# More places for the scheduler in a block pair, and a later earliest moment for the weighted sums of v, in a fused attention and feed-forward kernel

## The chip, the cores and the metric

The kernel runs on one core of one Trainium2 chip. The metric is the device time in microseconds, the median of several runs. TensorE is called PE here (its weight loads PEld), VectorE is DVE, ScalarE is ACT, GpSimd is POOL, and SyncE, which issues DMAs, is SP.

## The reference

Softmax attention over 8 batches, 12 heads, 448 positions and a head size of 64 is followed by a feed-forward layer with a leaky ReLU on the 3584 tokens that it gives:

```python
scores = np.matmul(q, k.transpose(0, 1, 3, 2)) / np.sqrt(64)      # q, k, v: (8, 12, 448, 64)
attn = np.exp(scores - scores.max(-1, keepdims=True))
attn = attn / (attn.sum(-1, keepdims=True) + 1e-09)
x = np.matmul(attn, v).transpose(0, 2, 1, 3).reshape(3584, 768)
h = x @ w_in                                                      # w_in: (768, 2048)
out = np.maximum(0.01 * h, h) @ w_out                             # w_out: (2048, 768)
```

## The kernel before

**Attention.** The work is cut into 48 units, each a pair of heads of one batch, and each unit into four chunks of 112 keys. `scores` (matmuls at L271) writes the scores of a chunk for both heads into one of three PSUM slots (`slots`, taken in turn by `next_slot`); `expo` (L280, ACT) reads the slot and writes the exponentials `e` to SBUF. `rows` is the weighted sum of v for a whole unit: 32 small matmuls (L789) into the next slot, then a reciprocal (L795) and a product (L796) on DVE. The rows of x that come of it are transposed by a DMA on SP's queue (`turn`, L237) into `xT`. `burst` issues the scores of three chunks and their exponentials, so it needs all three slots. GpSimd casts q, k and v for later units (L170, L172) and issues their loads (L141), and SP also transposes q and k (into `qkT`); `advance` issues one step of each, and what it may issue depends on `chunk` (chunks begun) and `rows_done` (units whose weighted sum is issued).

**Feed-forward.** The tokens are cut at `cuts` = 0, 640, 1152, 1664, 2176, 2688, 3072 and 3584 into seven stages. In each of stages 1 to 6 `hidden(i)` makes h by a seven-product scheme on halves of the matrices (matmuls at L469), and `second(i)` multiplies h by w_out in pairs of blocks of 128 tokens. `block_pair` does a pair with seven products of eight matmuls of 384 columns (L541), into two PSUM banks `b` and `a` in turn; each product is followed by a copy (`keep`, L546) or an addition (`join`, L549) that empties its bank, and the first two by a subtraction on h (L553, L558). In a stage of fewer than 512 tokens, and in the last one, the first copy of the first pair is done by ACT, all others by DVE. Stage 0 is different: its hidden part is `head` and `neck`, and its first pair is a `plain_pair` (L606).

**The sums on x.** The seven-product scheme of `hidden(i + 1)` wants sums and differences of x, which `mix_x_part` makes on DVE (L416): four subtractions for the first two of three parts of k, then four for the third. In the stage where the tokens begin at the start of `xT`'s ring (stage 3) six small copies (L404) go ahead of them. `hidden` needs the third of each four for its fifth and sixth group of matmuls. `second(i)` issues them between the products if it can: `fresh` is the moment of the planner's clock from which they may go, 7.0 after the weighted sums that they depend on were placed. What has not been issued by the end of the pairs is issued behind them. In `hidden` there is one slot for weighted sums, and two of them are issued in a stage, after the second and the sixth group of matmuls.

**The order.** All of it is fixed when the program is built. `block_pair` and `plain_pair` are generators that `yield` at places; at each place `second(i)` calls `place`, which decides by a small model of times (`model`: the clock `now`, ACT's end `act`, when each slot is `free`, when a unit's exponentials are `ready`) whether a burst or weighted sums are issued there. It tries a burst first, and then a weighted sum where `calm` allows. `plan` = 9, 8, 8, 8, 8, 5, 0 says how many bursts each stage does. The tests on the model are these:

```python
x <= now + 0.05 + 0.2 * j for j, x in enumerate(at)              # a burst, slots j = 0, 1, 2
at[0] <= now + 0.05 and ready.get(u, 0) <= now + 0.05            # a weighted sum of unit u
```

Of the kernel before, what the change touches and what calls it, by code (L numbers as in the profile page):

```python
# [16 lines left out]
def kernel(  # L17
# [20 lines left out]
    NU = B * HP  # L38
# [3 lines left out]
    NR = len(cuts) - 1  # L42
    HEAD = S
    need = [HP * -(-t // S) for t in cuts]
# [59 lines left out]
    MH = MD // 2  # L104
# [17 lines left out]
    for t in (w_in_mix, w_mix):  # L122
        t = t.rearrange("p x k n -> p (x k n)")
# [301 lines left out]
    def token(i, x):  # L425

        return KEEP * P if x == KEEP else cuts[i] + x * P
# [96 lines left out]
    def block_pair(i, c):  # L524

        lo, hi = slice(0, MH), slice(MH, MD)
        x1, x2 = spots(i)[1][c]
        one, two = ts(x1, P), ts(x2, P)
        s3 = h_mix[:, :, c]
        t2, t3, t4 = (w_mix[:, x] for x in range(3))  # L530
        t1 = w_out_sb[:, lo, NW:]
        left, right = slice(0, NW), slice(NW, DM)
        o1 = o_pool.tile([P, DM], F32, name="o")
        o2 = o_pool.tile([P, DM], F32, name="o")
        b, a = banks

        def product(ps, x, w, first=False, cols=slice(0, NW)):
            for m in range(MH):
                if m == MH // 2:
                    yield  # L540
                nc.tensor.matmul(  # L541
                    ps[:, cols], x[:, m], w[:, m], start=(first and m == 0), stop=(m == MH - 1), skip_group_check=True,
                )

        def keep(o, at, ps, by=nc.vector.tensor_copy):
            by(o[:, at], ps[:, :NW])  # L546

        def join(o, at, ps):
            nc.vector.tensor_add(o[:, at], o[:, at], ps[:, :NW])  # L549

        yield
        yield from product(b, h[:, lo, one], w_out_sb[:, lo, left], first=True)
        nc.vector.tensor_sub(h[:, lo, one], h[:, lo, two], h[:, lo, one])  # L553
        short = cuts[i + 1] - cuts[i] < 4 * P
        keep(o1, left, b, nc.scalar.copy if c == 0 and (short or i + 1 == NR) else nc.vector.tensor_copy)
        yield
        yield from product(a, h[:, hi, one], w_out_sb[:, hi, left], first=True)
        nc.vector.tensor_sub(h[:, hi, one], h[:, hi, one], h[:, lo, one])  # L558
        join(o1, left, a)
        yield  # L560
        yield from product(b, h[:, lo, one], t2)
        keep(o1, right, b)
        yield
        yield from product(a, h[:, lo, two], t1, first=True)
        keep(o2, right, a)
        yield
        yield from product(b, s3, t3)
        join(o2, right, b)
        yield
        t0 = token(i, x2)  # L570
        last = t0 + P == B * S
        if last:
            nc.vector.tensor_copy(o2[:, NW // 2:NW], b[:, NW // 2:NW])
            store(o1, token(i, x1), left)
            store(o2, t0, right)
        yield from product(a, h[:, hi, one], w_out_sb[:, hi, right])
        join(o1, right, a)
        store(o1, token(i, x1), right if last else slice(0, DM))
        yield
        if last:  # L580
            w1, w2 = slice(0, NW // 2), slice(NW // 2, NW)
            yield from product(b, h[:, hi, two], t4[:, :, w1], cols=w1)
            nc.vector.tensor_copy(o2[:, w1], b[:, w1])
            store(o2, t0, w1, (nc.scalar, nc.sync))
            end = slots[0][:, 0]
            yield from product(end, h[:, hi, two], t4[:, :, w2], first=True, cols=w2)
            nc.vector.tensor_add(o2[:, w2], o2[:, w2], end[:, w2])
            store(o2, t0, w2, (nc.scalar, nc.sync))
            return
        yield from product(b, h[:, hi, two], t4)  # L590
        keep(o2, left, b)
        store(o2, t0)
        banks.reverse()
# [276 lines left out]
    model = {"now": 0.0, "act": 0.0, "free": {}, "ready": {}}  # L870

    def place(i, want, soon=0, full=True, calm=True, first=False, lazy=0, keen=NU, cap=NU):

        free, ready = model["free"], model["ready"]
        done, state = 0, 0
        while True:
            settle_x(model["now"])
            now = model["now"]
            last = divmod(chunk + 2, NSC)[0]
            blocked = rows_done <= min(last, NU - 1) - NE  # L880
            u = rows_done
            whole = u < chunk // NSC
            at = [free.get(id(x), 0.0) for x in slots]
            u = to["pe"]
            if full and max(want, soon) > done and u <= min(last, NPE - 1) and state == 0:
                transposes(u)
                to["pe"] += 1
                state = 1
                model["now"] += 0.45
                continue  # L890
            if want > done and state < 2 and turned(last) and not blocked and len(slots) == 3 and all(
                x <= now + 0.05 + 0.2 * j for j, x in enumerate(at)
            ):
                state = 2
                order = list(slots)
                start = chunk
                burst(lazy)
                if first:
                    feed(start // 3)
                done += 1  # L900
                for x, t in enumerate(order[:chunk - start]):
                    model["act"] = max(model["act"], now + 0.45 + 0.2 * x) + 0.8
                    free[id(t)] = model["act"] + (0.15, 0.15 + 0.5 * (lazy > 1), 0.15 + 0.5 * lazy)[x]
                    if (start + x) % NSC == NSC - 1:
                        ready[(start + x) // NSC] = model["act"] + 0.1
                model["now"] = now + 0.78
                continue
            u = to["pe"]
            if first and full and state == 0 and u < min(NPE - 1, to["cast"] - 1) and u - NQ < chunk // NSC and model["act"] <= now + 0.6:
                transposes(u)  # L910
                to["pe"] += 1
                state = 1
                model["now"] += 0.45
                continue
            u = rows_done
            if calm and whole and not (lazy and late) and at[0] <= now + 0.05 and ready.get(u, 0) <= now + 0.05 and (
                u <= (chunk + 5) // NSC - NE or u < keen
            ) and u < cap:
                t = slots[0]
                rows()  # L920
                if first:
                    pay()
                model["now"] = now + 1.08
                free[id(t)] = now + 2.33
                continue
            return done

    def second(i):

        x_sums = [mix_x_part(i + 1, slice(0, 2)), mix_x_part(i + 1, slice(2, 3))] if i + 1 < NR else []  # L930
        fresh, summed = [None, None], [i + 1 == NR] * 2
        left = plan[i]
        for c in range(len(spots(i)[1])):
            whole = c < plain(i)
            for x, _ in enumerate((plain_pair if whole else block_pair)(i, c)):
                if x % 2 == 0:
                    advance()
                if c or x:
                    model["now"] += 0.65
                left -= place(i, left, calm=whole or x not in (1, 3), keen=need[min(i + 2, NR)], cap=NU if all(summed) else need[i + 2])  # L940
                if whole and x in (1, 3, 5, 7):
                    mix_h(i, x - 1)
                if whole and x in (8, 9, 11, 13, 15):
                    next(outs)
                if i == 0 and c and x % 2:
                    next(ins, None)
                for y in range(2):
                    if fresh[y] is None and i + 1 < NR and rows_done >= need[i + 2] - 1 + y:
                        fresh[y] = model["now"] + 7.0
                for y, todo in enumerate(x_sums):  # L950
                    if fresh[y] is not None and fresh[y] <= model["now"] and not summed[y]:
                        summed[y] = next(todo, 0) is not None
                        if not summed[y]:
                            break
        assert left == 0 or chunk == NU * NSC, (i, left)
        assert i + 1 == NR or rows_done >= need[i + 2], (i, rows_done)
        for todo in x_sums:
            for _ in todo:
                pass
# [62 lines left out]
```

## Time and profile before

| what | value |
|---|---|
| median of 3 runs | 392.66 us (391.87 to 393.14) |
| the profiled execution | 389.6 us, its span 387.8 us |
| PE busy | 379.8 us, 98% |
| ACT busy | 265.3 us, 68% |
| DVE busy | 234.2 us, 60% |
| POOL busy | 142.9 us, 37% |
| mean granted clock of PE | 0.995 |
| stage 0's block pairs | from 75.2 to 107.9 us |
| hidden parts of stages 1 to 6 start at | 107.9, 157.2, 206.5, 255.7, 305.0, 347.3 us |
| block pairs of stages 1 to 6 start at | 128.3, 177.6, 226.9, 276.1, 320.9, 365.7 us |

A line of the page names the engine, the line of the program and what is written and read. Matmuls overlap, so the time of one is read from start to start, and the duration shown for one is longer. The time "idle before" names what ended an engine's wait.

### The profile page before, as it was taken

To read this page: it belongs to the slowest core of one execution; us is meant where nothing else is said; L and a number is where in the kernel's file an instruction comes from. 1 tells how busy PE (TensorE), PEld (TensorE's weight loads), DVE (VectorE), ACT (ScalarE), POOL (GpSimd) and SP (SyncE) were. 2 spreads that over 40 slices of the span, in tenths; PEclk is the share of its full clock that TensorE was granted. 3 is DMA by queue.
4 is the path that set the end of the run, shared out by engine and by line. 5 is a ranking of instruction groups with operands and counts; after the bars stand their busy time and mean duration, and the time that the engine had idled before them with its cause. 6 is when DMAs were issued, how large, how long until landed. Compare 5 with 4: busy or idle time off the path is not lost.

```text
span 387.8 us, 10006 instructions
## 1 busy us (share of the span) xinstructions
PE 379.8 (98%) x4093; PEld 260.6 (67%) x4093; DVE 234.2 (60%) x489; ACT 265.3 (68%) x391; POOL 142.9 (37%) x222
## 2 busy tenths in 40 slices
PE   7899999999999999999999999999999999999996
PEld 3665657755588655886558865578655795568854
DVE  3564767575767646657466574575745665464854
ACT  6898885767747877587776877758776677708700
POOL 8798820876545443620435304354042000000000
PEclk9899999999999999999999999999999999999999
DMA  8999999899997958991599913999138600421023
GB/s 129 198 200 203 184 200 173 110 132 211 132 133 115 147 99 141 204 127 25 84 153 164 162 34 62 174 148 183 29 51 174 138 18 3 107 55 51 3 75 89
DMA packets 93246, 46.75 MB, mean 121 GB/s; under 512 B 51856, under 2 KB 89872, under 8 KB 93200
## 3 DMA queue, kind: packets, MB, share of 16 engines
q0 software_dynamic: 38224, 22.58, 47.6%
q1 hardware_dynamic: 54912, 23.50, 32.4%
q8 instruction: 32, 0.52, 0.6%
q14 instruction: 14, 0.11, 0.1%
q10 hardware_dynamic: 64, 0.02, 0.0%
HBM read 45.61 MB, written 11.01 MB: 146 GB/s over the span
## 4 chain that ended last, share of the span: by engine, by line
PE 92%; DMA 3%; DVE 2%; POOL 1%; issue 1%; ACT 1%; POOLq 0%; DVEq 0%; ACTq 0%
PE g L541 30%; PE g L469 14%; PE sc L469 14%; PE sc L789 11%; PE sc L271 10%; PE g L352 4%; PE g L606 3%; PE g L647 2%; PE g L290 2%; DMA w_in_mix<-in_k_dram 2%; DMA xT<-x 1%; PE g L254 1%; POOL w_in_mix L141 1%; PE sc L352 1%; PE g L317 1%
## 5 line engine op out<-in xcount | busy, mean ns | idle before, releaser
L280 ACT ACTIVATE e<-sc 112x896 bf16<-112x896 f32 x192 | 163.2, 918 | 48.2 <-PE sc L271 48.0
L541 PEld LDWEIGHTS <-h 128*128 128x128 bf16 x632 | 57.1, 98 | 45.0 <-issue 13.3
L541 PE MATMUL g<-w_out_sb,h 128*128 128x384 bf16 x416 | 78.7, 326 | 0.0
L458 ACT ACTIVATE h<-c 128x512 bf16<-128x512 f32 (+1 forms) x72 | 43.5, 611 | 25.8 <-DVE c L484 16.8
L469 PEld LDWEIGHTS <-w_in_sb 128*128 128x128 bf16 x576 | 54.3, 98 | 6.2 <-issue 0.3
L170 POOL COPY qkb<-fq 112x512 bf16<-112x512 bf16 x38 | 26.9, 707 | 72.1 <-DMA qkT<-qkb 32.1
L789 PEld LDWEIGHTS <-e 112*128 112x128 bf16 x1344 | 46.5, 98 | 8.7 <-ACT e L280 7.4
L172 POOL COPY v<-fv 112x512 bf16<-112x512 bf16 x38 | 25.2, 672 | 69.8 <-PE sc L789 69.0
L271 PE MATMUL sc<-qkT 64*128 64x448 bf16 x384 | 50.0, 356 | 0.9 <-DVE qkT L260 0.7
L789 PE MATMUL sc<-v,e 112*128 112x65 bf16 x1344 | 50.1, 194 | 0.4 <-ACT e L280 0.4
L469 PEld LDWEIGHTS <-w_in_mix 128*128 128x128 bf16 x432 | 41.2, 98 | 4.1
L541 PE MATMUL g<-w_mix,h 128*128 128x384 bf16 (+1 forms) x208 | 38.3, 323 | 0.2 <-DVE o L549 0.2
L546 DVE COPY o<-g 128x384 f32<-128x384 f32 x49 | 27.1, 553 | 18.6 <-PE g L541 18.0
L795 DVE RECIPROCAL rec<-sc 112x8 f32<-112x8 f32 x42 | 8.7, 207 | 46.3 <-PE sc L789 41.3
L271 PEld LDWEIGHTS <-qkT 64*128 64x128 bf16 x384 | 15.0, 94 | 26.3 <-issue 18.3
L170 POOL COPY qkb<-fk 112x512 bf16<-112x512 bf16 x38 | 25.1, 660 | 17.3 <-DMA fk<-in_k_dram 17.2
L549 DVE TENSOR_TENSOR o<-o,g 128x384 f32<-128x384 f32 x39 | 21.5, 551 | 15.0 <-PE g L541 14.9
L796 DVE TENSOR_TENSOR x<-sc,rec 112x512 bf16<-112x512 f32 x42 | 29.0, 691 | 1.5
L469 PE MATMUL g<-xT,w_in_sb 128*128 128x256 bf16 (+1 forms) x216 | 28.5, 268 | 0.1
L469 PE MATMUL sc<-xT,w_in_sb 128*128 128x256 bf16 (+1 forms) x216 | 28.5, 268 | 0.0
L541 PE MATMUL g<-w_mix,hmix 128*128 128x384 bf16 x104 | 19.9, 326 | 0.0
L469 PE MATMUL g<-x_mix,w_in_mix 128*128 128x256 bf16 (+1 forms) x144 | 19.0, 268 | 0.0
(102 smaller groups left out, 480.2 us busy)
## 6 DMA issues: line engine op xcount, KB each, us to landing
fq<-in_q_dram POOLq DMA_DIRECT2D x19, 224.0 KB, 6.7
fk<-in_k_dram POOLq DMA_DIRECT2D x19, 224.0 KB, 7.3
fv<-in_v_dram POOLq DMA_DIRECT2D x19, 224.0 KB, 5.9
w_in_sb<-in_moe_w_in_dram POOLq DMA_DIRECT2D x4, 768.0 KB, 11.6
w_out_sb<-in_moe_w_out_dram POOLq DMA_DIRECT2D x4, 768.0 KB, 18.6
out_dram<-o SPq DMA_DIRECT2D x7, 336.0 KB, 4.7
out_dram<-o SPq DMA_DIRECT2D x8, 288.0 KB, 3.5
out_dram<-o SPq DMA_DIRECT2D x7, 240.0 KB, 3.4
```

The costliest lines, as they stand in the source:

```text
L170: by(qk_sb[u][:, x].rearrange("p so h d -> p h so d"), f)
L172: by(v_sb[u % NV][:, :, :, :D], f)
L271: nc.tensor.matmul(ps[:, j, :S], t[j * D:(j + 1) * D, S + c * SC:S + c * SC + P], t[j * D:(j + 1) * D, :S], start=True, stop=True,)
L280: nc.scalar.activation(e[:, :, c, :], sc_t.pop((u, c))[:SC, :, :S], AX.Exp, scale=scale)
L352: nc.tensor.matmul(open_t[m][:, :n], w_in_sb[:, kk, ts(m, P)], xT[:, kk, at:at + n], start=(fresh and kk == kks[0]), stop=(kk == KD - 1),)
L458: nc.scalar.activation(hs[:, m:m + 2, cols], x.rearrange("p (m t) -> p m t", m=2), AX.Prelu, alpha=0.01)
L469: nc.tensor.matmul(ps[:, j * nh:(j + 1) * nh], w[:, kk, ts(j, P)], x[:, kk], start=(first and j == 0 and kk == 0), stop=(kk == KH - 1), sk ...
L541: nc.tensor.matmul(ps[:, cols], x[:, m], w[:, m], start=(first and m == 0), stop=(m == MH - 1), skip_group_check=True,)
L546: by(o[:, at], ps[:, :NW])
L549: nc.vector.tensor_add(o[:, at], o[:, at], ps[:, :NW])
L789: nc.tensor.matmul(ps[:, j, qc, :], e[:, at:at + P], vt[:, j, c, :], start=(c == 0), stop=(c == NSC - 1),)
L796: nc.vector.tensor_mul(x_t[u].rearrange("p q j d -> p j q d"), ps[:SC, :, :, :D], rec.to_broadcast([SC, 2, NSC, D]))
```

## The change

It has three parts. In `block_pair` a product yields ahead of its third, fifth and seventh matmul, where it yielded ahead of its fifth alone, so that a pair has 28 places in place of 14. `second(i)` is adapted to it: in block pairs the planner's clock advances by 0.325 at a place in place of 0.65, and `advance`, `ins`, the subtractions of `x_sums` and the places forbidden to weighted sums are bound to the new numbers of the places. In `place` the first slot of a burst is held free 0.3 after the model's end of its exponential, where it was 0.15; the weighted sum of v takes that slot.

```diff
@@ block_pair
         def product(ps, x, w, first=False, cols=slice(0, NW)):
             for m in range(MH):
-                if m == MH // 2:
+                if m in (2, 4, 6):
                     yield
@@ place
-                    free[id(t)] = model["act"] + (0.15, 0.15 + 0.5 * (lazy > 1), 0.15 + 0.5 * lazy)[x]
+                    free[id(t)] = model["act"] + (0.3, 0.15 + 0.5 * (lazy > 1), 0.15 + 0.5 * lazy)[x]
@@ second
             for x, _ in enumerate((plain_pair if whole else block_pair)(i, c)):
-                if x % 2 == 0:
+                fine = 1 if whole else 2
+                if x % (2 * fine) == 0:
                     advance()
                 if c or x:
-                    model["now"] += 0.65
-                left -= place(i, left, calm=whole or x not in (1, 3), keen=need[min(i + 2, NR)], cap=NU if all(summed) else need[i + 2])
+                    model["now"] += 0.65 / fine
+                left -= place(i, left, calm=whole or x > 8 or x % 4 == 0, keen=need[min(i + 2, NR)], cap=NU if all(summed) else need[i + 2])
...
-                if i == 0 and c and x % 2:
+                if i == 0 and c and x % 4 == 2:
                     next(ins, None)
...
-                for y, todo in enumerate(x_sums):
+                for y, todo in enumerate(x_sums if x % fine == 0 else ()):
                     if fresh[y] is not None and fresh[y] <= model["now"] and not summed[y]:
```

## The prediction

> **What bounds the kernel now.** I read the page's first and fourth parts, then the waits, then the timeline stage by stage. TensorE (PE) is busy for 98% of the span, and the chain that ended last is 92% PE, so a change pays only through gaps between matmuls.
>
> ```profile
> PE 379.8 (98%) x4093; PEld 260.6 (67%) x4093; DVE 234.2 (60%) x489; ACT 265.3 (68%) x391; POOL 142.9 (37%) x222
> ...
> PE 92%; DMA 3%; DVE 2%; POOL 1%; issue 1%; ACT 1%; POOLq 0%; DVEq 0%; ACTq 0%
> ```
>
> From the waits, the one gap that the change aims at (us in total, times, longest):
>
> ```profile
> PEld L789 <- ACT e L280: 7.4, 24, 0.5
> ```
>
> The timeline (start, duration, engine, line, count, idle time before) of stage 1 shows it: a burst, four matmuls, a weighted sum of v.
>
> ```profile
> 143.43 0.74 PE L271 MATMUL sc<-qkT 64*128 64x448 bf16 x6
> 143.90 2.53 ACT L280 ACTIVATE e<-sc 112x896 bf16<-112x896 f32 x3 [0.26 <-PE sc L271]
> ...
> 144.11 0.82 PE L541 MATMUL g<-w_out_sb,h 128*128 128x384 bf16 x4
> 144.87 1.07 PEld L789 LDWEIGHTS <-e 112*128 112x128 bf16 x32 [0.32 <-ACT e L280]
> 144.87 1.20 PE L789 MATMUL sc<-v,e 112*128 112x65 bf16 x32
> ```
>
> A matmul of L541 takes 0.1625 us start to start (40 of them 6.50 us in the chain), so the four from 144.11 end at 144.76, and the sum starts at 144.87: it waits 0.10 us for the first exponential to give up its PSUM slot. So read, 23 sums follow a burst by four matmuls in the pairs; 13 wait 0.10 and ten 0.044: stage 0 has four long ones, stages 1 to 4 two of either kind each, stage 5 one long and two short. That is 0.41 + 4 x 0.29 + 0.19 = 1.77 us, 0.5% of the run. Everything else in the pairs streams; each burst costs the same 0.77 us wherever it stands.
>
> **The planner, followed by hand.** Its own numbers give order only, no time. A burst at model time t frees its slots at t+1.25+m, t+2.20 and t+3.00 if ScalarE was idle (m: 0.15 before, 0.30 after); it advances the clock 0.78, a sum 1.08 (its slot is free 2.33 after its start), a place 0.65 before and 0.325 after. With the old numbers bursts of stage 1 stand at 1.30, 4.68, 8.49, 12.30, 15.03, 18.84, 22.65, 25.38 and sums at 6.11, 9.92, 16.46, 20.27. The trace has bursts at 129.71, 133.09, 136.89, 140.70, 143.43, 147.30, 151.17 and 153.90: the same distances, so the reading is right.
>
> With the new numbers bursts stand at 0.98, 4.68, 8.49, 12.30, 15.03, 17.76, 22.65, 25.38, sums at 6.44, 10.25, 19.52, 20.60. The third sum misses its place at 16.46, because the first slot is free at 16.58 (allowed: 16.51); the next quiet place is 17.76, where a burst is possible and goes first. Sums three and four then stand side by side at the end. Stages 2, 3 and 4 start from the same offsets of chunk and rows and repeat this; stage 5 (five bursts) has its last two sums at 17.76 and 18.84 in place of 16.46 and 18.84.
>
> **What it removes.** All 23 sums now come at least six matmuls after their burst, 0.325 us later, against waits of at most 0.10: 1.77 us saved. In stage 0 the first two sums join, bursts and the last sum slip, and one transpose of qkT is issued on SyncE's queue behind the x transpose of unit 16 in place of ahead of it. Before, that x transpose went out at 99.62, landed about 105.1, and its first subtraction held VectorE:
>
> ```profile
> 105.16 0.70 DVE L416 TENSOR_TENSOR x_mix<-xT 128x512 bf16<-128x512 bf16 x1 [1.04 <-DMA xT<-x]
> ...
> 106.37 1.46 PE L541 MATMUL g<-w_mix,h 128*128 128x384 bf16 x8 [0.22 <-DVE o L549]
> ```
>
> PE lost 0.38 us there (start gap 0.546 less 0.163) and 0.25 ahead of the next stage. About 3.5 us earlier on the queue, it lands in time: 0.63 saved. If it keeps its order on the queue, the last burst, now inside the waiting product, makes this +0.5 instead. Saved in all: 2.40.
>
> **What it moves to a worse place: the subtractions for the next stage.** `mix_x_part` gives eight of them, four for the first two rows of k and four for the third. They may start 7.0 model units after the sums are planned (`fresh`). Before, the first four ran between the last products, and only four were left (timeline around the end of stage 1, VectorE and the first PE product that needs them):
>
> ```profile
> 156.56 0.42 DVE L416 TENSOR_TENSOR x_mix<-xT,x_mix 128x512 bf16<-128x512 bf16 x1
> 157.38 0.56 DVE L546 COPY o<-g 128x384 f32<-128x384 f32 x1 [0.41 <-PE g L541]
> 157.86 0.28 DVE L416 TENSOR_TENSOR x_mix<-xT 128x256 bf16<-128x256 bf16 x1
> 158.17 0.29 DVE L416 TENSOR_TENSOR xT<-xT 128x256 bf16<-128x256 bf16 x1
> 158.50 0.29 DVE L416 TENSOR_TENSOR x_mix<-xT 128x256 bf16<-128x256 bf16 x1
> 158.82 0.70 DVE L416 TENSOR_TENSOR x_mix<-xT,x_mix 128x256 bf16<-128x256 bf16 x1
> ...
> 160.83 0.82 PE L469 MATMUL g<-x_mix,w_in_mix 128*128 128x256 bf16 x6
> ```
>
> After, both sums are planned by 21.68, so `fresh` is 28.68, and the stage's last place is 28.44: none runs in the loop, all eight come behind the last copy, in stage 5 too (26.92 against 26.10). VectorE works in order, so the sum, reciprocal and additions of the next stage queue behind them.
>
> Measured from the end E of the pairs (157.18): the chain starts at E+0.68, quiet it takes 4 x 0.455 + 4 x 0.325 = 3.12 (gaps of 0.035 included), and PE needs its seventh result at E+3.87: the product that reads x_mix starts at 160.83, and its third matmul 0.22 later. Quiet that is ready at E+3.5: no stall. But GpSimd's casts slow these instructions (timeline at the start of stage 4):
>
> ```profile
> 256.28 0.62 POOL L170 COPY qkb<-fk 112x512 bf16<-112x512 bf16 x1 [2.80 <-DMA fk<-in_k_dram]
> ...
> 256.40 0.64 DVE L416 TENSOR_TENSOR x_mix<-xT 128x256 bf16<-128x256 bf16 x1
> ...
> 257.07 0.71 DVE L416 TENSOR_TENSOR xT<-xT 128x256 bf16<-128x256 bf16 x1
> ```
>
> Beside GpSimd one takes 0.58 to 0.74, so eight take 3.1 to 5.5 us. In stages 2, 3 and 4 (the stage whose `hidden` part waits) GpSimd is at work there, though some subtractions slip through; I take the middle, 4.3. Then the seventh result comes near E+4.5, a stall of 0.65; the hidden stage's first sum leaves its slot near E+6.0, and the second, due at E+4.96 plus that stall, waits 0.4 more: 1.05 a stage. Stage 3 has six copies more (L404, 0.17 and a gap each, 1.2 us): 2.25. Stage 5 has narrower tiles and a cast or two: 0.4 to 0.85, taken 0.6, on the slot. Stage 6 has no GpSimd work and no sums to fill: needed at E+2.84, ready at E+3.52, 0.7. Together 1.05 + 2.25 + 1.05 + 0.6 + 0.7 = 5.65; all quiet 0 + 1.1 + 0 + 0.4 + 0.7 = 2.2; a walk with every subtraction beside GpSimd at 0.7 gives 1.6 + 2.5 + 1.7 + 0.85 + 0.7 = 7.35.
>
> The Trainium skill, "SBUF — State Buffer", section "SBUF: two separate sides", says that VectorE and GpSimd share one pair of ports by an exclusive lock, and the loser waits for the whole instruction. By that alone eight subtractions could wait a 0.62 us cast each, an estimate of 8.1 us a chain and some 11 us more in all; the rows of 0.58 to 0.74 show less than that, and they decide.
>
> **The first burst before the first copy.** It moves from the end of product 1 into it, so the copy out of bank b comes a burst (0.77) later than product 2 can cover. In stages 1 to 4 the subtraction L553 (0.69) and copy (0.55) end at E'+3.5 on the stage's own clock, and product 3 wants the bank at E'+3.38: 0.14 each, 0.56. In stage 5 that copy is ScalarE's, and goes behind three exponentials (timeline before, copy first):
>
> ```profile
> 322.41 0.48 ACT L546 COPY o<-g 128x384 f32<-128x384 f32 x1 [0.47 <-PE g L541]
> ...
> 322.79 2.54 ACT L280 ACTIVATE e<-sc 112x896 bf16<-112x896 f32 x3
> ...
> 324.29 1.46 PE L541 MATMUL g<-w_mix,h 128*128 128x384 bf16 x8
> ```
>
> Burst at 1.07, exponentials from 1.47 to 4.0, copy to 4.4, product 3 due at 3.38: 1.07 lost.
>
> **Edits at nothing.** More `yield`s emit no instruction. `advance`, `ins` and the weight subtractions keep their places. Casts of v follow the sums on GpSimd's queue by one tick (1.3 us) but are used a stage later. The x transposes of the late sums (median 4.6 us to landing) end before their subtractions; if not, the stall grows by the lateness. Sums now stand six matmuls ahead of the next burst in place of eight: their slot is needed 2.49 us after the sum's start and free at 2.28; cover 0.2.
>
> **Sum.** -2.40 + 5.65 + 0.56 + 1.07 = +4.9 us. The profiled execution took 389.6 (span 387.8), which becomes 394.5; the median 392.66 becomes 397.6.
>
> **Rivals.** (1) The subtractions still find places in the loop; it hangs on 0.24 model units (28.68 against 28.44), and for it speaks only that I may have missed a step. Then -2.40 + 0.56 + 1.07 = -0.8: 391.9, not slower. If the copy of stage 5 is covered as well, -1.84: 390.8. (2) The port stays quiet: -2.40 + 2.2 + 1.63 = +1.4: 394.1. (3) Every subtraction meets a cast: +6.6, 399.3. Against (2) and (3) speak mixed durations, 0.28 beside 0.70, in the same stretch.
>
> **How the numbers follow.** Forecast and (3) together 65% (the latter 15%), (2) 15%, (1) 12% and its better form 8%. The range goes from 393.0, under (2), to 400.0, over (3); some 13% lies below and 6% above. About 0.3% (1.2 us) can be told from no change. Faster 0.10: the better form and an edge of (1). Same 0.13: the rest of (1) and an edge of (2). Slower 0.77.
>
> **What would show it.** Right: no L789 wait on L280 in pairs; eight L416 in a row behind each last copy; PE gaps at the third product of a hidden stage, at its second sum, and 1.1 us in stage 5 ahead of product 3. Wrong: L416 between joins, no gap at those places.

## The result: slower by 1.3%, as forecast, though one term of the sum was too small

On one chip the kernel before took 391.16 us (median of 6 runs, 388.87 to 393.14) and the changed one 396.22 us (6 runs, 394.84 to 397.76). The ratio is 1.0134, with a 95% interval of 1.0084 to 1.0183. The profiled execution of the changed kernel took 396.07 us, its span 394.3 us, at a granted clock of 1.0.

The two lines of the page that answer to those of before: engine busy times, and the chain that ended last.

```profile
PE 379.1 (96%) x4093; PEld 261.8 (66%) x4093; DVE 236.4 (60%) x489; ACT 264.1 (67%) x391; POOL 141.2 (36%) x222
...
PE 86%; DVE 7%; issue 2%; DMA 2%; ACT 1%; POOL 1%; POOLq 0%; DVEq 0%; ACTq 0%
```

PE does the same work, but its share falls from 98% to 96%, and VectorE's share of the chain grows from 2% to 7%. The waits name the places (us in total, times, longest):

```profile
PE g L469 <- DVE x_mix L416: 3.3, 3, 1.7
...
PEld L789 <- DVE x L796: 2.3, 3, 1.4
...
PE g L469 <- DVE xT L404: 1.1, 2, 0.7
...
PE g L541 <- ACT o L546: 0.9, 1, 0.9
...
PEld L789 <- ACT e L280: 0.7, 2, 0.5
```

The last line was 7.4 us in 24 waits before: the waits in the pairs, at which the change aims, are gone (the two that are left stand elsewhere). The other four are new. The first three are PE in the hidden parts, held by the late subtractions L416, by a product L796 queued behind them, and by the copies L404 that stand ahead of them; the fourth is stage 5's copy on ScalarE.

The sizes below are PE's gaps: each start-to-start time less the usual one for that form. The timeline of the changed kernel at the start of stage 4 shows the largest:

```profile
258.36 0.56 DVE L546 COPY o<-g 128x384 f32<-128x384 f32 x1 [0.74 <-PE g L541]
...
258.83 0.77 DVE L416 TENSOR_TENSOR x_mix<-xT 128x512 bf16<-128x512 bf16 x1
...
260.37 0.70 POOL L141 DMA_DIRECT2D fv<-in_v_dram  x1 [0.30 <-POOL v L172]
260.38 0.43 DVE L416 TENSOR_TENSOR x_mix<-xT 128x512 bf16<-128x512 bf16 x1
...
260.84 2.15 DVE L416 TENSOR_TENSOR x_mix<-xT,x_mix 128x512 bf16<-128x512 bf16 x1
261.06 0.62 POOL L170 COPY qkb<-fq 112x512 bf16<-112x512 bf16 x1
...
261.61 0.62 POOL L170 COPY qkb<-fk 112x512 bf16<-112x512 bf16 x1
...
262.91 0.28 DVE L416 TENSOR_TENSOR x_mix<-xT 128x256 bf16<-128x256 bf16 x1
...
263.89 0.60 PE L469 MATMUL g<-x_mix,w_in_mix 128*128 128x256 bf16 x4 [1.71 <-DVE x_mix L416]
```

All eight subtractions come behind the last copy (four of them are shown). The fourth takes 2.15 us where 0.42 is usual, while GpSimd does two casts, and PE's third matmul on x_mix waits. At the start of stage 3 the copies L404 go first:

```profile
206.94 1.74 DVE L404 COPY xT<-xT 128x16 bf16<-128x16 bf16 x5
207.16 0.48 PE L469 MATMUL g<-xT,w_in_sb 128*128 128x256 bf16 x2 [0.73 <-DVE xT L404]
...
207.97 0.60 PE L469 MATMUL g<-xT,w_in_sb 128*128 128x256 bf16 x4 [0.34 <-DVE xT L404]
...
211.66 0.60 PE L469 MATMUL g<-xT,w_in_sb 128*128 128x256 bf16 x4 [1.19 <-DVE x_mix L416]
```

The copies do not only delay the subtractions: the first product of the hidden part reads what they write, and waits for them, 0.89 us ahead of its first matmul and 0.60 inside it.

### The profile page after: what moved, and what is told of

The parts are those of the page before. It is cut to its first block, busy times and chain, and to the rows that moved or that the text cites. A ratio compares the mean times of both kernels' runs of the same rounds, so it can differ in the third digit from the quotient of the medians.

```text
span 394.3 us, 10012 instructions
## 1 busy us (share of the span) xinstructions
PE 379.1 (96%) x4093; PEld 261.8 (66%) x4093; DVE 236.4 (60%) x489; ACT 264.1 (67%) x391; POOL 141.2 (36%) x222
## 4 chain that ended last, share of the span: by engine, by line
PE 86%; DVE 7%; issue 2%; DMA 2%; ACT 1%; POOL 1%; POOLq 0%; DVEq 0%; ACTq 0%
PE g L541 30%; PE sc L469 12%; PE g L469 11%; PE sc L271 10%; PE sc L789 10%; PE g L352 4%; DVE x_mix L416 3%; PE g L606 3%; PE g L647 2%; DMA w_in_mix<-in_k_dram 2%; PE g L290 2%; DVE xT L416 1%; PE g L254 1%; ACT e L280 1%; DVE x L796 1%
## 5 line engine op out<-in xcount | busy, mean ns | idle before, releaser
L172 POOL COPY v<-fv 112x512 bf16<-112x512 bf16 x38 | 25.1, 667 | 79.2 <-PE sc L789 79.2
L789 PEld LDWEIGHTS <-e 112*128 112x128 bf16 x1344 | 47.3, 98 | 6.5 <-DVE x L796 2.3
L789 PE MATMUL sc<-v,e 112*128 112x65 bf16 x1344 | 49.0, 194 | 1.9 <-DVE x L796 1.5
L170 POOL COPY qkb<-fq 112x512 bf16<-112x512 bf16 x38 | 25.4, 668 | 68.5 <-DMA fq<-in_q_dram 38.2
L796 DVE TENSOR_TENSOR x<-sc,rec 112x512 bf16<-112x512 f32 x42 | 29.0, 691 | 1.5
```

Of the source, the lines that this page charges most:

```text
L170: by(qk_sb[u][:, x].rearrange("p so h d -> p h so d"), f)
L172: by(v_sb[u % NV][:, :, :, :D], f)
L789: nc.tensor.matmul(ps[:, j, qc, :], e[:, at:at + P], vt[:, j, c, :], start=(c == 0), stop=(c == NSC - 1),)
L796: nc.vector.tensor_mul(x_t[u].rearrange("p q j d -> p j q d"), ps[:SC, :, :, :D], rec.to_broadcast([SC, 2, NSC, D]))
```

## The experiments

In all kernels of this section each DMA transpose of q, k and x is replaced by two plain copies of the same bytes, so the rows land untransposed and the attention is not the reference's. Nothing else differs where no edit is named. Ratios are to the kernel before, run on the same chip. The runs stand on four chips, on which the kernel before took 389.6 to 391.0 us; runs on different chips are compared by their ratios.

### The two kernels on plain copies

> The kernel before, with one thing left out: each DMA transpose (of x, q and k) is two plain DMA copies of the same bytes on SyncE's queue, so rows are not transposed. All further runs have this too, and this one is their base. All theories: instructions on the other engines are those of the kernel before; copies may land sooner or later than the transposes' 4.6 us median. Expected within 2 us of the kernel before; the first 75 us up to stage 0's pairs, where loads set the pace, can move.

> The changed kernel with plain copies in place of the transposes, to be compared with the base. Theory (VectorE's late subtractions and the first burst ahead of the first copy): the gaps of PE stay where the changed kernel has them, 7.5 us at the start of hidden stages 2 to 6 and 1.6 us ahead of product 3, less 1.8 us of waits of the sums: 5 to 7 us above the base. Rival (the late landing of the x transposes costs the time): copies land sooner, and the two are within 2 us.

Before: 388.7 us (10 runs), ratio 0.9963 (0.9937 to 0.9989). Changed: 395.31 us (4 runs), ratio 1.0135 (1.0085 to 1.0184). The difference, 6.6 us, has the places of the real pair: waits of 2.03, 2.97 and 0.95 us in the hidden parts of stages 2, 3 and 4 (1.50, 2.84 and 2.24 in the real pair; 1.5 of stage 3 at its first product), 0.46 and 0.54 in stages 5 and 6, 1.05 at product 3 of stage 5. In neither of the changed kernels does PE or a late subtraction wait for a transfer of x there. So the slowdown does not come from transposes of x that land late, and the pair is a base for what follows.

### Subtractions allowed earlier

```diff
-                        fresh[y] = model["now"] + 7.0
+                        fresh[y] = model["now"] + (4.0 if i else 7.0)
```

> The changed kernel (plain copies), but from stage 1 on the subtractions on x may start 4.0 planner units after the sums that they need, in place of 7.0, so that four of the eight stand between the last products again (three at the end of stage 5); bursts and sums stay where the change put them. Theory (late subtractions): the 7.5 us of gaps at the start of hidden stages 2 to 6 fall to under 0.7 us, the 1.6 us ahead of product 3 stay: 6 to 7.5 us under the changed kernel with plain copies, from 1 us under to 1 us over the base. Rival (the subtractions wait for the data of the late sums wherever they stand): the gaps move between the products, and less than 3 us is won.

388.14 us (8 runs), ratio 0.9951 (0.9923 to 0.9979), 7.2 us under the changed kernel. The waits in the hidden parts of stages 2 to 6 are gone; product 3 still waits 0.11 in stages 1 to 4 and 1.05 in stage 5. So the slowdown goes when the subtractions find their places in the loop again.

### The margin alone, in the kernel before

```diff
-                    free[id(t)] = model["act"] + (0.15, 0.15 + 0.5 * (lazy > 1), 0.15 + 0.5 * lazy)[x]
+                    free[id(t)] = model["act"] + (0.3, 0.15 + 0.5 * (lazy > 1), 0.15 + 0.5 * lazy)[x]
```

> The kernel before (plain copies) with the 0.3 alone; places stay at every fourth matmul. Theory (the later earliest moment delays the third and fourth sum of a stage, and with them the subtractions): seven or eight subtractions stand behind the last copy in stages 1 to 5, gaps of 5 to 7.5 us at the start of the hidden stages, 1.8 us of waits of the sums saved, none of the first burst's 1.6 us: 3.5 to 6 us above the base. Rival (the finer places are the cause): 1.8 us under the base.

A miss: 388.75 us (10 runs), ratio 0.9956 (0.9929 to 0.9984), no slower than its base, although seven or eight subtractions come late here too. Its timeline at the start of stage 2 (in the runs on plain copies lines stand two further down where no others are named; L418 is L416 of before):

```profile
155.32 0.41 DVE L418 TENSOR_TENSOR xT<-xT 128x512 bf16<-128x512 bf16 x1
155.77 0.42 DVE L418 TENSOR_TENSOR x_mix<-xT 128x512 bf16<-128x512 bf16 x1
156.23 0.42 DVE L418 TENSOR_TENSOR x_mix<-xT,x_mix 128x512 bf16<-128x512 bf16 x1
156.37 1.20 PE L791 MATMUL sc<-v,e 112*128 112x65 bf16 x32 [0.24 <-ACT e L282]
156.38 0.74 POOL L170 COPY qkb<-fq 112x512 bf16<-112x512 bf16 x1 [2.05 <-DMA fq<-in_q_dram]
156.58 0.70 DVE L418 TENSOR_TENSOR x_mix<-xT 128x256 bf16<-128x256 bf16 x1
...
157.40 0.82 PE L471 MATMUL g<-xT,w_in_sb 128*128 128x256 bf16 x6
```

GpSimd has one cast there. One subtraction takes 0.70 beside it, the others take their quiet 0.42 and 0.29, and PE waits for none of them: its 0.41 in each of stages 2, 3 and 4 (0.73 in stage 5) is a sum behind ScalarE's exponentials, because the last burst slipped. Only stage 6 waits 0.54 for a subtraction. Five of the six copies L404 kept a place in the loop. So being late is not enough. The question became what GpSimd does to a late subtraction.

### GpSimd's casts left out, then shortened, then added

First the casts of the units from 24 on were left out (their attention reads stale tiles). In this run and the next the buffers of the cast q and k are three fixed tiles taken in turn, `qk_static`, in place of a pool of three.

```diff
+            if u >= 24:
+                if x < 2:
+                    qk_sb[u] = qk_static[u % 3]
+                continue
```

> Changed kernel on plain copies without GpSimd's casts of q, k and v of the units from 24 on (their attention reads stale tiles); the order on PE, ACT and VectorE is the same, the subtractions are as late, GpSimd only issues loads. Theory, that lateness alone costs some 2 to 2.5 and the rest is VectorE held up beside GpSimd: the eight subtractions take 0.42 and 0.29 each, waits in the hidden parts of stages 2 and 4 fall from 2.0 and 0.95 to 0.4 or less, stage 3 keeps 1 to 2 because of its six copies; 391.5. Rival, that being late is enough by itself: waits as before, 394.5 to 395.3. Second rival, that DMAs of casts and loads hold the copies: also 394.5 or more.

The time is 398.96 us (5 runs), ratio 1.0262 (1.0224 to 1.03). That is a miss, and it has a reason of its own: a transfer into `qkT` kept PE waiting for 5.5 us in stage 1, and PE's clock fell after it. Perhaps the loads, which no cast held back any more, delayed it; no run tests that. The waits in the hidden parts of stages 2, 3 and 4, however, fell from 5.95 to 1.27 us, of which 1.1 is stage 3's first product. Since the transfers were disturbed too, the test was made again with the casts kept but cut to 8 of their 64 columns:

```diff
+            if u >= 24:
+                d = qk_sb[u][:, x].rearrange("p so h d -> p h so d") if x < 2 else v_sb[u % NV][:, :, :, :D]
+                by(d[:, :, :, :8], f[:, :, :, :8])
+                continue
```

> Changed kernel on plain copies; GpSimd's casts of q, k and v of the units from 24 on are cut to 8 of their 64 columns (the rest of the tiles is stale), so that they keep their number, their place on the queue and their waits, and the loads their pace. The subtractions are as late as in the changed kernel. Theory, that a late subtraction costs what GpSimd's casts add to it: each is beside a cast for 0.15 or so in place of 0.62; the waits in the hidden parts of stages 2, 3 and 4, 5.95 together with full casts, fall to 1.5 to 2.5 (stage 3 keeps 0.9 at its first product, which waits for copies at L404); 391 to 392. Rival, that it is the number of GpSimd's instructions or its DMA issues that hold VectorE, not the length of the casts: 394 or more.

391.02 us (11 runs), ratio 0.9998 (0.997 to 1.0027). By the ratios that is 1.4%, some 5 us, under the changed kernel on plain copies, and PE's gaps are 4.1 us in place of 9.3. Every engine has the instructions of that kernel in the same order in this run, so apart from the fixed tiles the length of the casts is all that differs. The timeline at the start of stage 2 (L423 is L416 of before, L172 the short cast):

```profile
156.51 0.24 POOL L172 COPY qkb<-fk 112x64 bf16<-112x64 bf16 x1 [2.32 <-DMA fk<-in_k_dram]
...
156.79 0.42 DVE L423 TENSOR_TENSOR x_mix<-xT 128x512 bf16<-128x512 bf16 x1
...
157.24 0.70 POOL L142 DMA_DIRECT2D fv<-in_v_dram  x1 [0.30 <-POOL v L172]
157.25 0.42 DVE L423 TENSOR_TENSOR xT<-xT 128x512 bf16<-128x512 bf16 x1
...
159.48 0.29 DVE L423 TENSOR_TENSOR x_mix<-xT,x_mix 128x256 bf16<-128x256 bf16 x1
159.51 0.35 POOL L172 COPY qkb<-fq 112x64 bf16<-112x64 bf16 x1 [1.57 <-DMA qkT<-qkb]
```

The eight run from 156.79 to 159.77 without a stretch, also beside the issue of a load (157.24). PE's waits in the hidden parts of stages 2 to 6 are 0, 1.08, 0, 0.15 and 0.54 us. What is left in stage 3 is the copies.

Then the reverse: to the kernel with the margin alone, four copies on GpSimd behind the last copy of stages 1, 2 and 3.

```diff
+        if i in (1, 2, 3) and c == len(spots(i)[1]) - 1:
+            nc.gpsimd.tensor_copy(s3[:, :4], o2[:, :512].rearrange("p (m n) -> p m n", m=4))
+            for x, y in ((4, 0), (0, 4), (4, 0)):
+                nc.gpsimd.tensor_copy(s3[:, x:x + 4], s3[:, y:y + 4])
```

> The kernel before on plain copies with margin 0.30 alone (388.75, with its subtractions late and GpSimd quiet there), and four copies of 128x512 on GpSimd behind the last copy of the pairs of stages 1, 2 and 3 (one from f32, three from bf16, some 2.5 us together, into a part of hmix that is dead by then). They fall on the late subtractions. Theory: subtractions of 0.42 and 0.29 become 0.6 to 2, waits in the hidden parts of stages 2, 3 and 4 grow from 0.41 each to 1 to 2 each, 390.5 to 393. Rival, that GpSimd's copies are not what holds the subtractions: 388.75.

390.12 us (11 runs), ratio 0.9988 (0.9955 to 1.0021): 0.3%, some 1.2 us, above the ratio without them, with intervals that overlap, and below the range expected. One reason is in the trace: in the first of the three stages the copies stood behind a cast that waited for its load, and met no subtraction. In stage 4 all met:

```profile
256.24 2.03 POOL L598 COPY hmix<-hmix 128x512 bf16<-128x512 bf16 x3
...
256.38 0.69 DVE L418 TENSOR_TENSOR x_mix<-xT 128x256 bf16<-128x256 bf16 x1
257.10 0.64 DVE L418 TENSOR_TENSOR xT<-xT 128x256 bf16<-128x256 bf16 x1
257.77 0.64 DVE L418 TENSOR_TENSOR x_mix<-xT 128x256 bf16<-128x256 bf16 x1
```

Subtractions of 0.29 take 0.64 to 0.69, and that stage's waits grow from 0.41 to 1.17 us. Where the copies met none, in stage 2, the wait stayed at 0.41. The time does not show the effect by itself; the trace of stage 4 does.

### The loads one step later on GpSimd's queue

In the traces of the kernels so far some subtractions take 1.2 to 2.15 us, and each of these began while GpSimd issued a load that had casts ready behind it, as the one at 260.84 above.

```diff
-        if tick % 2 == 0:
+        if tick % 2 == (tick > 14):
```

> Changed kernel on plain copies; from stage 1 on GpSimd issues each load of raw q, k and v one step later on its own queue (1.3 us), so that in the stretch of the late subtractions the cast of v is followed by the casts of q and k at once, and the loads come behind them. The order on PE, ACT, VectorE and SP is the same, the subtractions are as late, the casts as many. In the changed kernel and three others each subtraction of 1.2 to 2.15 us began while GpSimd issued a load, with casts ready behind it. Theory A, that such a start makes VectorE wait until GpSimd has done all its casts: none over 0.9 now, the wait of stage 2 falls from 2.0 to 0.5 to 1.2, stages 3 and 4 about as before (2.97 and 0.95); 393.5 to 394.5. Theory B, that it is casts back to back that hold VectorE, whatever is ahead of them: a subtraction of 1.5 us or more is still there, 395.

391.75 us (11 runs), ratio 1.0052 (1.0015 to 1.0088): by the ratios 0.8%, some 3 us, under the changed kernel on plain copies, with no other engine's order changed, and below the range that either theory gave. The waits of stages 2, 3 and 4 are 0.30, 2.06 and 0.61 us in place of 2.03, 2.97 and 0.95. The timeline at the start of stage 4:

```profile
258.05 0.61 POOL L170 COPY qkb<-fk 112x512 bf16<-112x512 bf16 x1 [2.19 <-DMA fk<-in_k_dram]
258.07 0.73 DVE L418 TENSOR_TENSOR xT<-xT 128x256 bf16<-128x256 bf16 x1
258.60 0.67 POOL L170 COPY qkb<-fq 112x512 bf16<-112x512 bf16 x1
258.84 0.58 DVE L418 TENSOR_TENSOR x_mix<-xT 128x256 bf16<-128x256 bf16 x1
259.22 0.67 POOL L170 COPY qkb<-fk 112x512 bf16<-112x512 bf16 x1
259.45 0.58 DVE L418 TENSOR_TENSOR x_mix<-xT,x_mix 128x256 bf16<-128x256 bf16 x1
```

Three casts back to back, and each subtraction waits for one of them only; none in this run is over 0.75 us. Theory B falls: casts back to back are not enough. Theory A does not hold as it was put either. In the kernels with full casts fifteen subtractions that began beside an issue with two casts right behind it were held, seven of them through both casts, and eight for 0.58 to 0.71 only (one in the changed kernel, stage 3, at 209.05). Others that began there were not held at all. The step also moved casts, some of them out of the stretch, so what the order alone gained is not shown. Why some starts are held through two casts stays open.

### The first burst, and the finer places alone

```diff
-        model.update(now=0.0, act=2.3, free={id(x): 0.9 for x in slots}, ready={})
+        model.update(now=0.0, act=2.3, free={id(x): 1.2 for x in slots}, ready={})
```

> Changed kernel on plain copies in place of the DMA transposes (rows land untransposed), with one edit more: the first slot counts as free only from 1.2 on at the start of a pair stage, so that the first burst of stages 1 to 5 comes after eight matmuls in place of six. My theory, that a burst inside product 1 delays the emptying of bank b: the waits at product 3 (0.114 in each of stages 1 to 4, 1.05 in stage 5) go, all waits in the hidden parts stay, and the time falls by 1.5 us from the 395.3 of the changed kernel on plain copies, to 393.8. Rival, that what stands at product 3 is only the first sign of a VectorE that is behind, and comes back at the next product: 395.3.

394.17 us (5 runs), ratio 1.015 (1.0098 to 1.0201). In the profile no product 3 waits any more in stages 1 to 5, 1.5 us less, and the subtractions stay late. The time fell by 1.1 us against another chip's 395.31, and the ratios do not separate the two: the place is shown, its worth only by the profile.

With the margin back at 0.15, the finer places alone:

> Changed kernel on plain copies with the slot's margin put back to 0.15: the finer places alone. Its sums stand four matmuls behind a burst again, and the third and the fourth apart. My theory: the subtractions find their old places, no wait of over 0.5 in a hidden part; sums wait 0.10 three or four times a stage (1.9 in all in place of 1.77), the first burst costs its 1.5; so 388.7 + 0.1 + 1.5 - 0.3 = 390.0. Rival, that the finer places delay the subtractions by themselves: 394 to 395.

389.62 us (11 runs), ratio 0.9997 (0.9963 to 1.0031). No wait in a hidden part; 0.12 at product 3 and 0.10 at one sum a stage, 1.04 in stage 5. So it is the margin of 0.30 that pushes the third sum behind a burst, and with it the subtractions out of the loop; the finer places cost only the first burst.

### Versions that keep the gain

Both repairs together (subtractions 4.0 after their sums, first slot free at 1.2):

> Changed kernel on plain copies, with both repairs: subtractions allowed 4.0 model units after their sums in place of 7.0, and the first burst after eight matmuls. My theory (terms add): 1.5 us under the 388.1 of the repair of the subtractions alone, so 386.6, which is 2 us under the 388.7 of the kernel before on plain copies: what the six matmuls between burst and sum were worth (1.77) and stage 0 (0.6). Rival, that the late first burst brings the third sum or its subtractions back behind the end: 389 or more.

386.2 us (7 runs), ratio 0.9912 (0.9871 to 0.9953). All of PE's gaps in the block pairs and hidden parts of stages 0 to 6 are 0.47 us together, against 3.1 in the kernel before on plain copies. The chain of the page:

```profile
PE 94%; DMA 2%; DVE 1%; POOL 1%; ACT 1%; issue 1%; POOLq 0%; DVEq 0%; ACTq 0%
```

With the first slot free at 1.2 here too, and a place more for the third sum in place of the smaller distance from the sums (the lines are cut at `...`):

```diff
-                left -= place(i, left, calm=whole or x > 8 or x % 4 == 0, ...
+                left -= place(i, left, calm=whole or x > 8 or x % 4 == 0 or (i > 0 and c == 1 and x == 5), ...
```

> Changed kernel on plain copies, the first burst after eight matmuls, and the third sum allowed one place more (six matmuls behind its burst, in the third product of the second pair), so that it stands alone and ahead of the burst again and the subtractions keep their old places without a smaller distance from their sums. My theory, that late sums were the only reason for late subtractions: no wait over 0.2 in a hidden part, 386.2 as with both repairs. Rival, that with 7.0 from the sums the last four subtractions still come late and cost 0.5 or so a stage in 2 to 5: 387.5 to 388.5.

387.21 us (5 runs), ratio 0.9898 (0.9845 to 0.9952), and no wait in the hidden parts of stages 2 to 6; 0.81 is lost in stage 0, where an addition stood behind a subtraction. So the third sum's place alone decides whether the subtractions are late. Both versions beat the changed kernel clearly. Against the kernel before on plain copies (0.9963) they gain some 0.5%, at the edge of what the intervals tell apart; with the transposes they were not run.

## Why the prediction was right, point by point

| step | predicted, us | PE's gaps in the profile after, us |
|---|---|---|
| waits of 23 sums | -1.77 | -1.77, all gone |
| stage 0's two gaps | -0.63 | -0.63, and 0.49 new |
| first burst, stages 1 to 4 | +0.56 | +0.59 |
| first burst, stage 5 | +1.07 | +1.04 |
| late subtractions, stage 2 | +1.05 | +1.50 |
| stage 3 | +2.25 | +2.84 |
| stage 4 | +1.05 | +2.24 |
| stage 5 | +0.6 | +0.46 |
| stage 6 | +0.7 | +0.54 |
| others (start of stage 1, one burst's slot) | 0 | +0.21 |
| sum | +4.9 | +7.5 |

The span grew by 6.5, not 7.5, since stage 0 began at 74.14 in place of 75.19 us, ahead of all that the change touches. The medians differ by 5.1. That this is so close to 4.9 is luck: the gaps say 7.5, the pair on plain copies 6.6, and the kernel before was profiled below its median (389.6 against 391.16), the changed one at it.

**What held.** The order that the planner gives, with the third sum missing its place and all subtractions behind the last copy, stands in the trace as predicted, and it carried the sign. The first burst's two costs are right to 0.03. In stage 5 ScalarE does the three exponentials first:

```profile
327.32 2.53 ACT L280 ACTIVATE e<-sc 112x896 bf16<-112x896 f32 x3 [0.44 <-PE sc L271]
329.72 0.49 ACT L546 COPY o<-g 128x384 f32<-128x384 f32 x1
...
330.27 1.46 PE L541 MATMUL g<-w_mix,h 128*128 128x384 bf16 x8 [0.88 <-ACT o L546]
```

The bound for a quiet GpSimd, 0, 1.1, 0, 0.4 and 0.7 for stages 2 to 6, is near what the short casts measured: 0, 1.08, 0, 0.15 and 0.54. The first rival (subtractions in the loop, 0.8 under before) is the run with earlier subtractions, 0.6 under its base.

**What was mis-sized.** The term for late subtractions came to 7.58 in place of 5.65. That is above even the 7.35 of the walk with every subtraction beside GpSimd, on which the third rival stands. Two steps of it failed. "Beside GpSimd one takes 0.58 to 0.74" was a row of one cast; the changed kernel has rows of 1.49 and 2.15, held through two casts, and these made stages 2 and 4. And the casts of v "one tick later" were put at nothing because they "are used a stage later": the cover was for whoever reads v, while the cast itself moved into the stretch of the subtractions. In stage 1 of before both casts of v stand ahead of the last copy:

```profile
152.42 1.17 POOL L172 COPY v<-fv 112x512 bf16<-112x512 bf16 x2
```

The changed kernel has one of them among the subtractions, ahead of the load beside which the fourth of the narrow ones begins:

```profile
157.98 0.80 POOL L172 COPY v<-fv 112x512 bf16<-112x512 bf16 x1
...
159.08 0.70 POOL L141 DMA_DIRECT2D fv<-in_v_dram  x1 [0.30 <-POOL v L172]
...
159.61 1.49 DVE L416 TENSOR_TENSOR x_mix<-xT,x_mix 128x256 bf16<-128x256 bf16 x1
```

No run takes this cast away alone, so its own share is not shown. In stage 3 it was missed that the first product reads what the copies L404 write (1.49 of the 2.84).

**Stage 0.** The x transpose came in time, as predicted, but a subtraction on h took 1.07 us in place of 0.69, and a product waited for the addition behind it:

```profile
96.14 1.07 DVE L558 TENSOR_TENSOR h<-h 128x1024 bf16<-128x1024 bf16 x1 [0.50 <-PE g L541]
...
97.72 0.48 PE L541 MATMUL g<-w_out_sb,h 128*128 128x384 bf16 x2 [0.33 <-DVE o L549]
```

**The rule weighed.** The Trainium skill, "SBUF — State Buffer", section "SBUF: two separate sides", has VectorE and GpSimd lock each other out for a whole instruction. The runs agree in kind: beside back-to-back casts of 0.61 to 0.67 a subtraction of 0.29 takes 0.58 to 0.73. They show less than a whole cast there, 0.29 to 0.44 us more than the quiet time, which fits a subtraction that arrives during a cast and waits for what is left of it; and more than one cast in the long rows. The estimate of 11 us from it was too high, my middle too low.

## What to carry to other kernels

A margin in a planner is priced by the place that the delayed step can take next: here 0.07 model units cost a sum its place, and the work that hung on that sum lost its cover. When work moves to where it is exposed, list what every other engine will be doing in that stretch after the change, also those whose moved work nobody waits for: they can still slow it. Being late cost about 2 us here with short casts beside it (1.8); with full ones it was 7.

## What the runs showed of the hardware that was not expected

A subtraction on VectorE can be held through more than one of GpSimd's instructions. In six kernels of this case, eight subtractions took 1.19 to 2.15 us where 0.29 or 0.42 is usual. Each began while GpSimd issued a load with one cast (the 1.19) or two (the others) right behind it, and ended after the last of these casts. With the loads issued behind the casts none was over 0.75. The issue of a load by itself slowed no subtraction (0.42 beside it). The start does not settle it: eight subtractions with the same two casts ready were held for 0.58 to 0.71 only. Those that waited for both casts began 0.35 to 0.60 us into the issue and left both casts at 0.62; the eight began 0.20 to 0.40 into it, and one or both of their casts took 0.67 to 0.88. That is a pattern in fifteen rows; no run tested it as a cause.

PE's clock halved after a long wait. In the run without casts PE was idle for most of 151 to 157 us, and the granted clock (the column PEclk, last but two) was 0.50 over the next 6.2 us:

```profile
151.00:157.00 6.00, 0.56 (x5) 0.12 (x4) 1.11 (x2) 1.99 (x3) 2.10 (x3) 0.98 1.35 194
157.00:163.20 6.20, 6.14 (x19) 2.62 (x20) 0.55 (x1) 0.92 (x1) 2.10 (x3) 0.50 1.37 183
163.20:180.00 16.80, 16.80 (x199) 15.19 (x198) 11.67 (x25) 11.10 (x21) 0.00 (x0) 0.99 0.70 135
```

Sixteen matmuls of 384 columns started 0.32 us apart there in place of 0.1625. After the waits of the hidden parts, up to 1.94 us, the granted clock stayed at 1.00. The Trainium skill, "TensorE: Matmul & The Clock Gate", section "What's actually happening", gives a free-running window of about 3.4 us: an idle one halves the clock, a busy one restores it. The 6.2 us here are longer than one such window; they fit if the first busy stretch was only part of one, which no run tests.
